# Attention with a two-layer network behind it on one core: first and last pair of a batch in another order, float32 value sums in one batch, other steps for w_out

## The chip, the cores and the metric

The kernel runs on 1 core of one Trainium2 chip. The metric is the device time of one execution in microseconds; the number for a kernel is the median of its runs. The times shown for the kernel before are 1271.4, 1273.9 and 1270.87 us, median 1271.4.

## The reference

Inputs are q, k, v of 8 batches, 12 heads, 448 rows, 64 columns, and the weights w_in (768 x 2048) and w_out (2048 x 768), all float32.

```python
scores = scale * np.matmul(q, k.transpose(0, 1, 3, 2)) - np.log(S)   # scale = 1/sqrt(64)
attn = 1.0 / (1.0 + np.exp(-scores))
x = np.matmul(attn, v).transpose(0, 2, 1, 3).reshape(B * S, H * D)
h = x @ w_in
g = np.where(h > 0.0, h, np.exp(np.minimum(h, 0.0)) - 1.0)
out = g @ w_out
```

So each head's scores go through a sigmoid, not a softmax, the heads' sums stand side by side as 768 columns for each of 3584 tokens, and a layer pair with the ELU function follows.

## The kernel before, in words

**Numbers as pairs of words.** Matrix products run in float16 with two words a number: `split` (L121 on ScalarE, L122 on VectorE) writes hi = float16(scaled source) and lo = float16(scaled source − hi). A product is then the sum of three: hi·hi, lo·hi, hi·lo. The scales are powers of two, found from a maximum: VectorE takes a maximum by row (`absmax`, L125), puts it on a diagonal `dg` (L105), TensorE spreads the diagonal over all partitions by a product with ones (`pb`, L110), and VectorE reduces that (`al`, L112 and on). In `magnitude`, the part up to `dg` is issued at once and the part from `pb` on is returned as `rest`, to be issued later.

**Work of a batch.** A batch is 6 pairs of heads (hp 0 to 5; n = 6 b + hp numbers all pairs) and then the network's first layer. Batches are numbered from 0. For each pair: `load_qk` and `load_v` (DMAs issued by SyncE into `raw` and `rv`), `prepare` (maxima, `dg`), its `second` part (`pb` and the scales `sc`), its `third` part (`transposed`: splits q and k to `nat`, a DMA transpose into `qk`, splits v to `vn`), `scores` of 4 tiles g (L384; tiles 0 to 2 have 128 keys, tile 3 has the last 64), `soften` (sigmoid to `sg`, L395, then for tiles 0 to 2 the two words `at`, L413 on ScalarE and L414 on VectorE), `values` (sum over keys into `pav`, L433 in words, L425 in float32 for the last tile), `finish` (two words of the result into `xh`). Tiles 0 and 1 and tiles 2 and 3 share two PSUM buffers `psc`, so the scores of tile 2 wait until the sigmoid of tile 0 is through, and those of tile 3 for tile 1. Then `hidden`: `rescale`, and `moe1` with 16 tiles f of 18 products (`ph`, L499), the exponential on ScalarE (L511), and the words of g. The change of ScalarE's function table between exponential and sigmoid is an instruction on ScalarE.

**Batch 0 and the weights.** Batch 0 takes its attention in float32 throughout. Its instructions are ordered by a scheduler. Beside it w_in is loaded and turned into words; beside its `moe1` the same goes on for w_out, by `load_w_out`, a generator of 64 steps: for each half i of the columns 16 load steps (DMA of one tile `so` or `wo`, L226; conversion by L138 and L142 on ScalarE, L143 and L157 on VectorE; a product with ones for the tile's maximum, `so`, L150) and 16 split steps (L121 and L122). `W_OUT = 4` steps stand behind each tile f from 2 on and one more behind the last: 57 steps. The other 7 stand in batch 1: three in each of pairs 0 and 1, the rest in pair 2. `step(n)` takes n of them. Tiles that can't be loaded into a part of `wo` that is still free go to three buffers `so` (tag `at`, which later holds the words of the attention).

**Batches 1 to 7** are written out by hand: on TensorE, ScalarE, VectorE and SyncE instructions stand in the order of the program; only GpSimd's are scheduled. TensorE waits in its order, so whatever stands behind a waiting instruction waits too. The second layer of the batch before (`moe2`: tiles `po` of 16 steps, a step is three products of 384 columns, L529) fills the places where the attention would wait: `fill(n)` takes n steps. There are 96 steps in odd batches and 128 in even ones (with the left-over rows of two batches), and each pair's share is what is left, divided by the pairs left. The row of a pair is: scores and soften of tiles 0 and 1, `third` of the next pair, loads of pair n+3, a gap of 5 steps (8 in pair 0), `prepare` of pair n+2, scores and soften of tiles 2 and 3, the rest of the share, `second` of pair n+2, values, finish. In the last pair (hp 5) `hidden` starts ahead of the fill, and 4 steps of the share, the tail, stand behind finish, ahead of `moe1`.

Of the kernel before, what the change touches and what calls it, by code (L numbers as in the profile page):

```python
# [32 lines left out]
def attention_ffn(  # L33
# [25 lines left out]
    SKEW = 2  # L59
    W_IN = [1, 3, 6, 9, 12, 15, 16]  # L60
    W_LOAD = [1, 1]
    W_OUT = 4
    assert 2 * D == P and 2 * R == P and NK == NP

    const = ctx.enter_context(tc.tile_pool(name="const", bufs=1))
# [54 lines left out]
    def split(hi, lo, src, s):  # L120
        nc.scalar.mul(hi, src, s)  # L121
        nc.vector.scalar_tensor_tensor(lo, src, s, hi, op0=ALU.mult, op1=ALU.subtract)  # L122
# [5 lines left out]
    def words(st):  # L128
        w = st.bitcast(U32).rearrange("p a (c t) -> p a c t", t=2)
        return w[:, :, :, 0], w[:, :, :, 1], st  # L130
# [71 lines left out]
    def load_w_out(wo):  # L202


        for i in range(NH):
            whole = [
                wo[:, i, f + SKEW].rearrange("p j c -> p (j c)").bitcast(F32)
                for f in range(NF - SKEW)
            ] + [
                sb.tile([P, HM], F32, tag="o", name=f"to{i}_{f}", bufs=OB) for f in range(SKEW)  # L210
            ]
            sums = ps.tile([P, 512], F32, tag="pm", name=f"so{i}", bufs=3)
            for f in range(NF):

                if i == 0 and f >= 2:
                    st = wo[:, 1, f % 8 * 2 :][:, :2]
                elif i == 1 and f % 2 and f < NF - SP - SKEW:
                    st = wo[:, 1, NF - SP + f // 2 % 2 * 2 :][:, :2]
                else:
                    st = None  # L220
                if st is None:

                    st = sb.tile([P, 1, HM], U64, tag="at", name=f"so{i}_{f}", bufs=AB)
                else:
                    st = st.rearrange("p a j c -> p (a j c)").bitcast(U64).unsqueeze(1)
                nc.sync.dma_start(  # L226
                    st[:, 0], w_out[f * P : (f + 1) * P, i * HM : (i + 1) * HM]
                )
                lo, hi, hl = words(st)
                t = whole[f].unsqueeze(1)  # L230
                magnitudes(t, lo, hi, hl, sums[:, :HM], f == 0, f == NF - 1)
                signed(t, hi)
                yield
            sum_magnitude(wop[:, i : i + 1], sums[:, :HM])
            s = sb.tile([P, 1 + NF], F32, tag="swo", name=f"swo{i}", bufs=2)
            nc.vector.reciprocal(s[:, 0:1], wop[:, i : i + 1])
            nc.vector.tensor_scalar(s[:, 1:], wn, s[:, 0:1], None, op0=ALU.mult)
            for f in range(NF):
                split(wo[:, i, f, 0], wo[:, i, f, 1], whole[f], s[:, 1 + f : 2 + f])
                yield  # L240
# [53 lines left out]
    def prepare(b, hp, raw, rv, xs):  # L294


        u = f"{b}_{hp}"
        n = 1 if b < EXACT else 3
        mx = sb.tile([P, 3], F32, tag="mx", name=f"mx{u}", bufs=2)
        absmax(mx[:, 0:1], rv.rearrange("p t d -> p (t d)"))  # L300
        if n > 1:
            mt = sb.tile([P, 2, NC + 1], F32, tag="mt", name=f"mt{u}", bufs=2)
            absmax(
                mt.rearrange("p i t -> p (i t)")[:, : 2 * NC + 1],
                raw.rearrange("p t h d -> p t (h d)"),
            )
            nc.vector.tensor_reduce(mx[:, 1:3], mt[:, :, :NC], axis=AX.X, op=ALU.max)
            for i, r in enumerate(rows):
                m = mx[r, 1 + i : 2 + i]
                nc.vector.tensor_tensor(m, m, mt[r, 0, NC:], op=ALU.max)  # L310
        pw = sb.tile([P, n], F32, tag="pw", name=f"pw{u}", bufs=2)
        product = magnitude(pw, mx[:, :n], n)

        def scales():
            product()
            sc = sb.tile([P, n + 3], F32, tag="sc", name=f"sc{u}", bufs=3)
            if b >= EXACT:
                nc.vector.reciprocal(sc[:, :n], pw)
                nc.gpsimd.tensor_scalar(sc[:, :n], sc[:, :n], 2.0**TOP, None, op0=ALU.mult)

                for i, r in enumerate(rows):
                    nc.gpsimd.tensor_copy(sc[r, n + 1 : n + 2], sc[r, 1 + i : 2 + i])

                nc.gpsimd.tensor_scalar(  # L324
                    sc[:, n + 2 :], pw[:, 1:2], pw[:, 2:3], 2.0 ** (-2 * TOP) / math.sqrt(D),
                    op0=ALU.mult, op1=ALU.mult,
                )
            value_scale(b, hp, pw[:, 0:1], sc[:, n : n + 1], xs)
            return lambda: transposed(sc)

        def transposed(sc):
            x_scale, s_rest, s_scale = (sc[:, n + i : n + i + 1] for i in range(3))
            if b < EXACT:
                pt = ps.tile([P, 2, 512], F32, tag="psc", name=f"pt{u}", bufs=2)
                pt = pt.rearrange("p a x -> p (a x)")
                for t in range(2 * NC + 1):
                    nc.tensor.transpose(
                        pt[:, t * P : (t + 1) * P], raw[:, t].rearrange("p h d -> p (h d)"), ident
                    )
                qk = early[:, hp % 2]  # L340
                nc.vector.tensor_copy(qk, pt[:, : 2 * S])
                return x_scale, 1 / math.sqrt(D), [qk], ([rv], rv[:, 2 * NC :])
            nat = sb.tile([P, 2, 2 * NC + 1, P], F16, tag="nat", name=f"nat{u}")
            for t, n_t, s in (
                (0, NC, sc[:, 1:2]), (NC, 1, s_rest), (NC + 1, NC, sc[:, 2:3])
            ):
                split(
                    nat[:, 0, t : t + n_t], nat[:, 1, t : t + n_t],
                    raw[:, t : t + n_t].rearrange("p t h d -> p t (h d)"), s,
                )  # L350
            qk = sb.tile([P, 2, 2 * NC + 1, P], F16, tag="qk", name=f"qk{u}", bufs=2)
            nc.sync.dma_start_transpose(
                qk.rearrange("p i t x -> p (i t) x"), nat.rearrange("p i t x -> p (i t x)")
            )
            parts = [qk[:, i].rearrange("p t x -> p (t x)") for i in range(2)]

            vn = sb.tile([P, 2, 2 * NC, D], F16, tag="vn", name=f"vn{u}", bufs=2)
            split(vn[:, 0], vn[:, 1], rv[:, : 2 * NC], sc[:, 0:1])
            vr = sb.tile([P, 2, D], F32, tag="vr", name=f"vr{u}", bufs=2)
            nc.gpsimd.tensor_scalar(  # L360
                vr, rv[:, 2 * NC :], sc[:, 0:1], 2.0**ATOP, op0=ALU.mult, op1=ALU.mult
            )
            return x_scale, s_scale, parts, ([vn[:, 0], vn[:, 1]], vr)

        return scales

    class Pair:
# [23 lines left out]
        def soften(self, g):  # L391
# [6 lines left out]
            if b - 1 in last_exp:  # L398
# [5 lines left out]
                    ),  # L404
                    reason="one change of tables each way for a batch",
                )
            if b < EXACT or g == NC:

                self.sg[g] = [sg]
                return  # L410
# [205 lines left out]
    def w_out_beside(f):  # L616
        nonlocal wo, steps
        if f == 0:
            w_in_ratios()
            wo = sb.tile([P, NH, NF, 2, HM], F16, tag="wo", name="wo")  # L620
            steps = load_w_out(wo)
        if f >= 2:
            step(W_OUT)
        if f == NF - 1:
            step(1)

    def pair_of(n):
        b, hp = pairs[n]
# [56 lines left out]
    with tc.manual_schedule(engines={E.PE, E.Activation, E.DVE, E.SP}):  # L685
        for b in range(EXACT, B):
# [9 lines left out]

            for hp in range(NP):
                n = b * NP + hp
                share = left // (NP - hp)
                tail = 4 if hp == NP - 1 else 0  # L700
                p = pair_of(n)
                for t in range(2):
                    p.scores(t)
                    p.soften(t)
                third()
                if n + 3 < len(pairs):
                    loaded[n + 3] = load_qk(*pairs[n + 3]), load_v(*pairs[n + 3])

                gap = 8 if hp == 0 else 5
                fill(gap)  # L710
                second = prepare_pair(n + 2)
                for t in range(2, NC + 1):
                    p.scores(t)
                    p.soften(t)
                if b == EXACT and hp < NC:

                    step(3 if hp < NC - 1 else NF)
                if hp == NP - 1:
                    h = hidden(b)
                    next(h)  # L720
                fill(share - gap - tail)
                third = second()
                for t in range(NC + 1):
                    p.values(t)
                p.finish()
                fill(tail)
                if b == EXACT and hp == NC - 1:
                    out_scale(*of_moe2, slice(1, NH))
            of_moe2 = next(h)
# [33 lines left out]
```

## Time and profile before

| what | value |
|---|---|
| median of the three runs | 1271.4 us |
| the profiled execution's own time | 1270.86 us |
| its span in the profile | 1269.1 us |
| TensorE busy (instructions) | 1200.2 us (7246) |
| VectorE busy | 823.4 us (1872) |
| ScalarE busy | 671.8 us (1015) |
| GpSimd busy | 84.1 us (319) |
| HBM read, written | 58.20 MB, 11.01 MB |

The span starts with the first instruction in the profile and ends with the last; 1.8 us of the execution's time lie outside it. In the profile PE is TensorE, DVE VectorE, ACT ScalarE, POOL GpSimd and SP SyncE; PEld is TensorE's loading of weights, beside its products. A row of a timeline gives the start, the busy time, the engine, the line of the code, the operation, output and inputs with their partitions and elements, the number of such instructions in a row (x24), and in square brackets the idle time of the engine ahead of them with the instruction that ended it. A row of waits gives the waiting instruction, the one it waited for, the total in us, how many times, and the longest. A row of the windows gives the stretch, its length, busy time and instructions of PE, PEld, DVE, ACT and POOL, the clock that TensorE was granted as a share of full speed, the busy share of the DMA engines and GB/s. SPq rows are DMAs as SyncE issued them; the row of a DMA group ends with the KB of one and the median us from issue to landing.

### The profile page before, as it was taken

Reading aid. Unit: us, or ns where it says so; the run is one execution under the profiler, and the core shown is the slowest. Engines: PE = TensorE matmul, PEld = TensorE weight load, DVE = VectorE, ACT = ScalarE, POOL = GpSimd, SP = SyncE. Lnnn points to the kernel's source line nnn. Section 1 sums busy time; section 2 is a strip of 40 time slices with the busy share of each in tenths; the row PEclk is TensorE's granted clock in tenths of the full one; section 3 lists DMA queues with packets and bytes.
Section 4 is the critical chain, followed back from the end, with each engine's and each line's share of the span. In section 5 each row is a group of like instructions: output and inputs, shape, how many; then the busy total and the mean of one; then the engine's idle time right before and its main releaser. Section 6 shows DMA issues by size and latency. Waiting matters only on the chain.

```text
span 1269.1 us, 19337 instructions
## 1 busy us (share of the span) xinstructions
PE 1200.2 (95%) x7246; PEld 610.5 (48%) x7246; DVE 823.4 (65%) x1872; ACT 671.8 (53%) x1015; POOL 84.1 (7%) x319
## 2 busy tenths in 40 slices
PE   5979868999999999999999999999999999999998
PEld 2324334445555554545455554545455554455565
DVE  5898989765766557775666646885576656765500
ACT  5867777643655337744555436654565435663400
POOL 0011001100000000010000000010000100100000
PEclk9889979999999999999999999999999999999999
DMA  8937423420233103340144201440034401410000
GB/s 229 281 100 222 126 77 80 100 49 1 60 84 89 37 1 83 89 86 1 37 92 92 50 1 43 105 103 7 1 86 92 92 1 22 106 43 7 1 25 26
DMA packets 213407, 89.76 MB, mean 71 GB/s; under 512 B 177472, under 2 KB 209216, under 8 KB 213312
## 3 DMA queue, kind: packets, MB, share of 16 engines
q1 hardware_dynamic: 213312, 88.51, 28.7%
q8 instruction: 57, 0.93, 0.3%
q14 instruction: 38, 0.31, 0.1%
HBM read 58.20 MB, written 11.01 MB: 55 GB/s over the span
## 4 chain that ended last, share of the span: by engine, by line
PE 78%; ACT 8%; DVE 7%; DMA 3%; issue 2%; SPq 2%; DVEq 0%; POOL 0%; ACTq 0%; POOLq 0%
PE ph L499 31%; PE po L529 25%; PE psc L384 7%; PE pav L433 6%; PE po_r L529 5%; PE pav L425 3%; ACT sg L395 2%; DMA stage<-in_moe_w_in_dram 2%; ACT at L413 1%; SPq L262 1%; PE pb L110 1%; ACT L395 1%; ACT e L511 1%; DVE e L514 1%; DMA so<-in_moe_w_out_dram 1%
## 5 line engine op out<-in xcount | busy, mean ns | idle before, releaser
L499 PE MATMUL ph<-xh,wi 128*128 128x448 f16 x2304 | 442.0, 353 | 6.1 <-DVE xh L122 2.4
L529 PE MATMUL po<-wo,g 128*128 128x384 f16 x2304 | 392.9, 328 | 0.0
L529 PEld LDWEIGHTS <-g 128*128 128x128 f16 x2688 | 257.2, 98 | 198.4 <-issue 36.3
L499 PEld LDWEIGHTS <-wi 128*128 128x128 f16 x2304 | 225.3, 98 | 218.4 <-issue 7.6
L511 ACT ACTIVATE e<-ph,msc 128x448 f32<-128x448 f32 x128 | 80.8, 633 | 211.7 <-PE ph L499 211.6
L414 DVE SCALAR_TENSOR_TENSOR at<-sg,at 128x896 f16<-128x896 f32 x126 | 137.2, 1090 | 84.5 <-ACT at L413 84.5
L395 ACT ACTIVATE sg<-psc,bias,sc 128x896 f32<-128x896 f32 (+1 forms) x168 | 166.6, 992 | 1.7
L513 DVE TENSOR_SCALAR e<-e 128x448 f32<-128x448 f32 x128 | 50.3, 394 | 170.8 <-ACT e L511 170.7
L121 ACT ACTIVATE xh<-pav,sc 128x448 f16<-128x448 f32 x48 | 30.3, 632 | 216.7 <-PE pav L425 216.7
L384 PE MATMUL psc<-qk 64*128 64x448 f16 x1008 | 116.6, 355 | 11.4 <-ACT sg L395 11.4
L413 ACT ACTIVATE at<-sg 128x896 f16<-128x896 f32 x126 | 119.8, 951 | 4.1
L121 ACT ACTIVATE g<-e,msc 128x384 f16<-128x384 f32 (+1 forms) x192 | 96.0, 534 | 6.0 <-DVE e L514 4.3
L122 DVE SCALAR_TENSOR_TENSOR g<-e,msc,g 128x384 f16<-128x384 f32 (+1 forms) x192 | 94.6, 521 | 0.6
L514 DVE SCALAR_TENSOR_TENSOR e<-ph,msc,e 128x448 f32<-128x448 f32 x128 | 87.3, 683 | 4.0
L384 PEld LDWEIGHTS <-qk 64*128 64x128 f16 x1008 | 41.7, 97 | 89.7 <-issue 60.2
L433 PE MATMUL pav<-at,vn 128*64 128x448 f16 x756 | 80.2, 357 | 0.0
L324 POOL TENSOR_SCALAR sc<-pw 128x1 f32<-128x1 f32 x42 | 12.4, 295 | 843.5 <-DVE pw L114 790.9
L529 PE MATMUL po_r<-wo,g 128*128 128x384 f16 x384 | 64.7, 326 | 0.0
L122 DVE SCALAR_TENSOR_TENSOR xh<-pav,sc,xh 128x448 f16<-128x448 f32 x48 | 32.7, 680 | 48.7 <-ACT xh L121 48.7
L433 PEld LDWEIGHTS <-vn 128*64 128x64 f16 x756 | 39.4, 110 | 50.0 <-issue 27.8
L122 DVE SCALAR_TENSOR_TENSOR nat<-raw,sc,nat 128x384 f16<-128x384 f32 (+1 forms) x126 | 59.1, 524 | 0.0
L121 ACT ACTIVATE nat<-raw,sc 128x384 f16<-128x384 f32 (+1 forms) x126 | 58.8, 529 | 0.0
(103 smaller groups left out, 852.7 us busy)
## 6 DMA issues: line engine op xcount, KB each, us to landing
stage<-in_moe_w_in_dram SPq DMA_DIRECT2D x16, 768.0 KB, 6.6
raw<-in_q_dram SPq DMA_DIRECT2D x96, 96.0 KB, 3.1
raw<-in_k_dram SPq DMA_DIRECT2D x96, 96.0 KB, 2.6
rv<-in_v_dram SPq DMA_DIRECT2D x48, 192.0 KB, 2.7
out_dram<-o SPq DMA_DIRECT2D x48, 192.0 KB, 2.1
wo<-in_moe_w_out_dram SPq DMA_DIRECT2D x19, 384.0 KB, 4.1
so<-in_moe_w_out_dram SPq DMA_DIRECT2D x13, 384.0 KB, 4.3
raw<-in_q_dram SPq DMA_DIRECT2D x48, 32.0 KB, 2.4
```

The costliest lines, as they stand in the source:

```text
L121: nc.scalar.mul(hi, src, s)
L122: nc.vector.scalar_tensor_tensor(lo, src, s, hi, op0=ALU.mult, op1=ALU.subtract)
L384: nc.tensor.matmul(psc[:, j, :S] if g < NC else psc[rows[j], 0, :S], kk[rows[j], o], qq[rows[j], :S], start=(n == 0), stop=(n == len(parts ...
L395: a = nc.scalar.activation(sg[:, :nb], psc[:, :nb, :S], AF.Sigmoid, bias=bias, scale=self.s_scale)
L413: nc.scalar.mul(hi, sg, 2.0**ATOP)
L414: nc.vector.scalar_tensor_tensor(lo, sg, 2.0**ATOP, hi, op0=ALU.mult, op1=ALU.subtract)
L433: nc.tensor.matmul(pav[rows[j], :S], vv[i][:, j * NC + g], sg[k][:, j], start=(g == 0 and n == 0), stop=False,)
L499: nc.tensor.matmul(ph[:, :S], wi[:, wj, c, f * P : (f + 1) * P], xh[:, c, xj], start=(n == 0), stop=(n == 3 * NK - 1),)
L511: a = nc.scalar.activation(e, ph[:, :S], AF.Exp, scale=inv)
L513: nc.vector.tensor_scalar(e, e, 1.0, -1.0, op0=ALU.min, op1=ALU.add)
L514: nc.vector.scalar_tensor_tensor(e, ph[:, :S], inv, e, op0=ALU.mult, op1=ALU.max)
L529: nc.tensor.matmul(po[:, :HM], lh(gj, f), wo[:, i, f, wj], start=(n == 0), stop=(n == 3 * NF - 1),)
```

## The change

It has four parts, in the diff below without its repeated lines.

- **w_out.** `W_OUT` is 3 and the extra step is gone: 42 steps stand in batch 0 and 22 in batch 1 (four after the gap and four after tiles 2 and 3 in pairs 0 and 1; four and the rest in pair 2). The load of a tile is issued two steps ahead of its conversion.
- **Values of batch 1.** For b = 1 the sigmoid stays float32, v is scaled by ScalarE alone into float32 `vn`, and `values` takes one product a half (6 a pair, recorded as 12) instead of three (18). No `at` is written there.
- **Pair 0 of each batch.** Its share has three steps more and its gap is 11. `prepare` of pair n+2 stands behind scores and soften of tiles 2 and 3, and its `second` (with `pb`) in the next pair, between the scores and the soften of tiles 0 and 1.
- **Last pair.** There is no tail: the whole share stands ahead of `second` and values.

By the share's rule odd batches now take 19, 15, 15, 15, 16, 16 steps and even ones 24, 20, 21, 21, 21, 21.

```diff
-    W_OUT = 4
+    W_OUT = 3
...
+            def load(f):
...
                 nc.sync.dma_start(
                     st[:, 0], w_out[f * P : (f + 1) * P, i * HM : (i + 1) * HM]
                 )
-                lo, hi, hl = words(st)
+                return st
+
+            staged = [load(f) for f in range(2)]
+            for f in range(NF):
+                if f + 2 < NF:
+                    staged.append(load(f + 2))
+                lo, hi, hl = words(staged[f])
...
+            if b == EXACT:
+                s_whole = sb.tile([P, 1], F32, tag="s2", name=f"s2{u}", bufs=2)
+                nc.gpsimd.tensor_scalar(s_whole, sc[:, 0:1], 2.0**ATOP, None, op0=ALU.mult)
+                vn = sb.tile([P, 2 * NC, D], F32, tag="vn", name=f"vn{u}", bufs=2)
+                nc.scalar.mul(vn, rv[:, : 2 * NC], s_whole)
+                return x_scale, s_scale, parts, ([vn], vr)
...
-            if b < EXACT or g == NC:
+            if b <= EXACT or g == NC:
...
-        if f == NF - 1:
-            step(1)
...
-                share = left // (NP - hp)
-                tail = 4 if hp == NP - 1 else 0
+                share = left // (NP - hp) + (3 if hp == 0 else 0)
                 p = pair_of(n)
                 for t in range(2):
                     p.scores(t)
+                if hp == 1:
+                    third = second()
+                for t in range(2):
                     p.soften(t)
                 third()
...
-                gap = 8 if hp == 0 else 5
+                gap = 11 if hp == 0 else 5
                 fill(gap)
-                second = prepare_pair(n + 2)
+                if b == EXACT and hp < NC:
+
+                    step(4)
+
+                if hp:
+                    second = prepare_pair(n + 2)
                 for t in range(2, NC + 1):
                     p.scores(t)
                     p.soften(t)
+                if not hp:
+                    second = prepare_pair(n + 2)
                 if b == EXACT and hp < NC:
-
-                    step(3 if hp < NC - 1 else NF)
+                    step(4 if hp < NC - 1 else NF)
...
-                fill(share - gap - tail)
-                third = second()
+                fill(share - gap)
+                if hp:
+                    third = second()
                 for t in range(NC + 1):
                     p.values(t)
                 p.finish()
-                fill(tail)
```

Two places where this moves instructions. The first is SyncE's row at the start of batch 1; `so` are tiles of w_out, `qk_1` is the transpose for pair 1, `raw_3` and `rv` are q, k and v of pair 3. Before:

```order
L226 DMA so_11_1476<-in_moe_w_out_dram 128x384
L226 DMA so_12_1507<-in_moe_w_out_dram 128x384
L226 DMA so_13_1514<-in_moe_w_out_dram 128x384
L226 DMA so_14_1521<-in_moe_w_out_dram 128x384
L226 DMA so_15_1528<-in_moe_w_out_dram 128x384
L352 DMA_TRANSPOSE qk_1_1648<-nat_1_1641 128x14x128
L262 DMA raw_3_1655<-in_q_dram 128x3x64 x2
L266 DMA raw_3_1655<-in_q_dram 64x2x64
L262 DMA raw_3_1655<-in_k_dram 128x3x64 x2
L266 DMA raw_3_1655<-in_k_dram 64x2x64
L247 DMA rv_85<-in_v_dram 128x2x192
L252 DMA rv_85<-in_v_dram 64x64 x2
```

And now, in the changed kernel:

```order
L227 DMA so_11_1540<-in_moe_w_out_dram 128x384
L359 DMA_TRANSPOSE qk_1_1580<-nat_1_1573 128x14x128
L269 DMA raw_3_1588<-in_q_dram 128x3x64 x2
L273 DMA raw_3_1588<-in_q_dram 64x2x64
L269 DMA raw_3_1588<-in_k_dram 128x3x64 x2
L273 DMA raw_3_1588<-in_k_dram 64x2x64
L254 DMA rv_85<-in_v_dram 128x2x192
L259 DMA rv_85<-in_v_dram 64x64 x2
L227 DMA so_12_1632<-in_moe_w_out_dram 128x384
L227 DMA so_13_1639<-in_moe_w_out_dram 128x384
L227 DMA so_14_1646<-in_moe_w_out_dram 128x384
L227 DMA so_15_1653<-in_moe_w_out_dram 128x384
```

The loads of the tiles 12 to 15 have moved from ahead of the transpose of pair 1 to behind it and behind the loads of pair 3.

The second place is VectorE's row in pair 0 of batch 3; the number behind a name's first underscore is the pair: `mx_2`, `mt_2` and `pw_2` belong to the preparation of pair 2, `at_0` and `xh` to pair 0. Before:

```order
L122 SCALAR_TENSOR_TENSOR vn_1_4696<-rv_85,sc_1_4205,vn_1_4696 128x384
L125 TENSOR_REDUCE mx_2_4736<-rv_83 128x1
L125 TENSOR_REDUCE mt_2_4738<-raw_2_4090 128x7
L307 TENSOR_REDUCE mx_2_4736<-mt_2_4738 128x2
L310 TENSOR_TENSOR mx_2_4736<-mx_2_4736,mt_2_4738 64x1 x2
L105 TENSOR_SCALAR dg<-eye,mx_2_4736 128x128 x3
L414 SCALAR_TENSOR_TENSOR at_0_4757<-sg_0_4755,at_0_4757 128x896
L537 TENSOR_SCALAR o_0_0_4793<-po_0_0_4711,osc_4659 128x384
L112 TENSOR_REDUCE al<-pb 128x3
```

Now:

```order
L122 SCALAR_TENSOR_TENSOR vn_1_4578<-rv_85,sc_1_4101,vn_1_4578 128x384
L427 SCALAR_TENSOR_TENSOR at_0_4634<-sg_0_4632,at_0_4634 128x896
L125 TENSOR_REDUCE mx_2_4646<-rv_83 128x1
L125 TENSOR_REDUCE mt_2_4648<-raw_2_3973 128x7
L314 TENSOR_REDUCE mx_2_4646<-mt_2_4648 128x2
L317 TENSOR_TENSOR mx_2_4646<-mx_2_4646,mt_2_4648 64x1 x2
L105 TENSOR_SCALAR dg<-eye,mx_2_4646 128x128 x3
L550 TENSOR_SCALAR o_0_0_4673<-po_0_0_4591,osc_4539 128x384
L122 SCALAR_TENSOR_TENSOR xh_3810<-pav_0_4686,sc_0_3903,xh_3810 128x448
L125 TENSOR_REDUCE xs_3811<-xh_3810 128x1
L112 TENSOR_REDUCE al<-pb 128x3
```

The words of the third tile (`at_0`) have moved ahead of the maxima and `dg`, and the reduction of `pb` behind the end of the pair (`xh`).

More of the change, by code (lines that the diff above doesn't have):

```diff
@@ L212, in load_w_out @@
             sums = ps.tile([P, 512], F32, tag="pm", name=f"so{i}", bufs=3)
-            for f in range(NF):
+            def load(f):
                 if i == 0 and f >= 2:
@@ L355, in transposed @@
             parts = [qk[:, i].rearrange("p t x -> p (t x)") for i in range(2)]
-            vn = sb.tile([P, 2, 2 * NC, D], F16, tag="vn", name=f"vn{u}", bufs=2)
-            split(vn[:, 0], vn[:, 1], rv[:, : 2 * NC], sc[:, 0:1])
             vr = sb.tile([P, 2, D], F32, tag="vr", name=f"vr{u}", bufs=2)
@@ L362, in transposed @@
             )
+            if b == EXACT:
[4 more added lines that the diff above has]
+                return x_scale, s_scale, parts, ([vn], vr)
+            vn = sb.tile([P, 2, 2 * NC, D], F16, tag="vn", name=f"vn{u}", bufs=2)
+            split(vn[:, 0], vn[:, 1], rv[:, : 2 * NC], sc[:, 0:1])
             return x_scale, s_scale, parts, ([vn[:, 0], vn[:, 1]], vr)
```

## The prediction

> **What bounds the kernel now.** I read the page first: the busy times and the shares of the chain that ended last.
>
> ```profile
> PE 1200.2 (95%) x7246; PEld 610.5 (48%) x7246; DVE 823.4 (65%) x1872; ACT 671.8 (53%) x1015; POOL 84.1 (7%) x319
> ...
> PE 78%; ACT 8%; DVE 7%; DMA 3%; issue 2%; SPq 2%; DVEq 0%; POOL 0%; ACTq 0%; POOLq 0%
> ```
>
> PE is busy for 1200.2 us of the 1269.1 us span, so about 69 us of it are idle, and 78% of the chain is PE's own work. The change removes no PE work in the steady part; it can only remove PE waits, and it may add some. So the next view is PE's waits in the window 268 to 1148 us (the stages of batches 2 to 7; batches are numbered from 0, pairs of a batch too):
>
> ```profile
> PE pb L110 <- DVE dg L105: 9.7, 5, 2.0
> PE psc L384 <- ACT sg L395: 6.7, 6, 1.2
> ```
>
> That is 16.4 us in eleven waits. PE's timeline shows where they stand:
>
> ```profile
> 260.77 0.32 PE L110 MATMUL pb<-dg,ones 128*128 128x384 bf16 x1 [1.90 <-DVE dg L105]
> ...
> 474.24 4.07 PE L529 MATMUL po<-wo,g 128*128 128x384 f16 x24
> ...
> 480.01 0.76 PE L384 MATMUL psc<-qk 64*64 64x448 f16 x6 [1.03 <-ACT sg L395]
> ...
> 486.75 0.32 PE L110 MATMUL pb<-dg,ones 128*128 128x384 bf16 x1 [1.97 <-DVE dg L105]
> ...
> 494.92 5.54 PE L529 MATMUL po<-wo,g 128*128 128x384 f16 x33
> 500.40 0.32 PE L110 MATMUL pb<-dg,ones 128*128 128x384 bf16 x1
> ```
>
> The psc wait (480.01) stands once in each of the six batches, in its first pair: the eight gap steps (24 po matmuls) don't last until the sigmoid of the second tile is through. The pb wait stands in the first pair of batches 3, 5, 7 (486.75) and in the last pair of odd batches (260.77 is batch 1's, ahead of the window). A step is three po matmuls; the 33 that start at 494.92 fill the time up to 500.40, so one step is 5.48/11 = 0.50 us.
>
> **The change part by part.**
>
> *Waits that go.* In the first pair the gap grows from 8 to 11 steps: 1.5 us more cover, over waits of 1.2 at most. The row max and dg now stand behind the second half of the sigmoids on DVE, and pb moves into the next pair, behind its first scores, several us after dg. The first pair also takes three steps more, so values find their operands. In the last pair the four tail steps move ahead of pb: 4 x 0.50 = 2.0 us of cover over waits of 1.90. All three kinds go: 6.7 + 9.7 + 1.9 = −18.3 us.
>
> *What is late next.* Three steps more in the first pair, and four that no longer trail the last one, leave less for the others: by the share rule the odd batches' pairs take 19, 15, 15, 15, 16, 16 steps where all took 16; even batches 24, 20, 21 and on. Pair 1 of batch 3, whose second fill is the 33 po at 494.92, has 16 steps, and there DVE's row reads:
>
> ```profile
> 499.77 0.58 DVE L105 TENSOR_SCALAR dg<-eye,mx 128x128 bf16<-128x128 bf16 x3
> ```
>
> dg ends at 500.35 and pb starts at 500.40: no slack, with DVE the later one. One step less and PE arrives 0.50 early and waits it out: three pairs (1 to 3) in each of batches 3, 5, 7: 9 x 0.50 = +4.5. With 20 or 21 steps an even batch has 2 us in hand. In the last pair the tail also covered the end of the stage:
>
> ```profile
> 265.11 0.67 DVE L122 SCALAR_TENSOR_TENSOR xh<-pav,sc,xh 128x448 f16<-128x448 f32 x1
> ```
>
> ```profile
> 265.65 3.57 PE L499 MATMUL ph<-xh,wi 128*128 128x448 f16 x18
> ```
>
> The last operand of the next matmuls, xh, was ready (265.78) about when ph started. Without the tail ph starts as soon as values end, and xh of the last pair is read only by the last 3 of 18 matmuls, 15 x 3.57/18 = 3.0 us in. xh follows the end of values by some 1.4 to 3 us in these rows, so the end is covered within a few tenths. I put +1.0 on these edges over all batches. Together +5.5 us; bounds 0 (DVE work pulled ahead by the same amount) and +9.
>
> *float32 values in batch 1.* The saved low word's split and the two forms of the values' sum:
>
> ```profile
> L414 DVE SCALAR_TENSOR_TENSOR at<-sg,at 128x896 f16<-128x896 f32 x126 | 137.2, 1090 | 84.5 <-ACT at L413 84.5
> ```
>
> ```profile
> 45.09 2.48 PE L433 MATMUL pav<-sg,rv 128*64 128x448 f32 x12
> ...
> 206.38 1.89 PE L433 MATMUL pav<-at,vn 128*64 128x448 f16 x18
> ```
>
> A pair drops three L414, 3 x 1.09 = 3.3 us of DVE, and their three first words on ACT, which once w_out is done nothing on PE waits for. PE pays 2.48 − 1.89 = 0.59 a pair, x6 = +3.5 us. The first row is batch 0's form at full clock, which batch 1 will issue. At half clock a group would cost up to twice as much, bound +10. The Trainium skill, page "FP8 and Floating Point Precision", section TensorE Precision Notes, says that true FP32 takes 4 passes through the array; 24 passes against 18 would be an estimate of 1.89 x 24/18 = 2.52, in this kernel +3.8, which speaks against this part of the change by 0.3 us more. The row decides.
>
> *Pair 1 of batch 1.* Before, twelve splits of w_out stood ahead of its sigmoids on ACT:
>
> ```profile
> 196.46 0.74 PE L384 MATMUL psc<-qk 64*128 64x448 f16 x6 [2.51 <-ACT sg L395]
> 198.43 1.17 PE L384 MATMUL psc<-qk 64*64 64x448 f16 x6 [1.23 <-ACT sg L395]
> 199.53 6.75 PE L529 MATMUL po<-wo,g 128*128 128x384 f16 x33
> ```
>
> Now the first steps there follow scores and sigmoids. The waits of 2.51 and 1.23 go, and with them the slow spell that makes 33 po take 6.75 instead of 5.54: −2.5 − 1.2 − 1.2 = −4.9. If the splits only move to pair 2 some of it returns: bounds −4.9 and 0.
>
> *Pair 0 of batch 1.* This is the disputed place. Before:
>
> ```profile
> 168.69 0.80 PE L150 MATMUL so<-wo,ones 128*128 128x384 bf16 x2 [1.42 <-DVE wo L143]
> 170.15 0.33 PE L150 MATMUL so<-wo,ones 128*128 128x384 bf16 x1 [0.67 <-DVE wo L143]
> 175.79 0.48 PE L150 MATMUL so<-wo,ones 128*128 128x384 bf16 x1 [5.30 <-DVE wo L143]
> 177.67 0.48 PE L150 MATMUL so<-to,ones 128*128 128x384 bf16 x1 [1.41 <-DVE to L143]
> 178.73 0.48 PE L150 MATMUL so<-to,ones 128*128 128x384 bf16 x1 [0.58 <-DVE to L143]
> 180.17 1.33 PE L384 MATMUL psc<-qk 64*64 64x448 f16 x6 [0.96 <-ACT sg L395]
> 181.43 5.80 PE L529 MATMUL po<-wo,g 128*128 128x384 f16 x24
> ```
>
> Idle: 1.42 + 0.67 + 5.30 + 1.41 + 0.58 + 0.96 = 10.3 us, on the loads of so_12 and later. In the order of instructions these loads stood on SP ahead of the transpose of pair 1; now so_12 to so_15 stand behind it and behind the loads of pair 3:
>
> ```profile
> 183.70 1.56 SPq L352 DMA_TRANSPOSE qk<-nat  x1
> ...
> 190.48 1.14 SPq L252 DMA_DIRECT2D rv<-in_v_dram  x2
> ```
>
> ```profile
> so<-in_moe_w_out_dram SPq DMA_DIRECT2D x10, 384.0 KB, 3.8
> ```
>
> From the transpose's start to the end of the last rv issue SP takes 191.62 − 183.70 = 7.9 us. Call T0 the end of batch 0's last ph. The transpose needs nat, whose splits follow two sigmoids on ACT; without the w_out work between them I put nat at T0 + 6, so so_12 is issued at T0 + 14 and lands at T0 + 18. PE has 11 steps (5.5 us) until its four so matmuls, then waits in order: some 13 us, 1.1 for the next tile's conversion (178.73 − 177.67) and 3.0 for so_15, whose buffer is so_12's and whose load goes out only then. That is 17.2, +6.9 against before; the half clock that follows such a gap is there before too (24 po in 5.80). Bounds: 0 and +11.
>
> *End of batch 0.* Two conversions fewer stand among its last tiles, and one wait of PE with the half clock behind it can go:
>
> ```profile
> 152.93 0.50 PE L150 MATMUL so<-wo,ones 128*128 128x384 bf16 x2 [2.07 <-DVE wo L143]
> ```
>
> I take −2, bounds −4 and 0.
>
> **Sum:** −18.3 + 5.5 + 3.5 − 4.9 + 6.9 − 2.0 = −9.3. The profiled execution took 1270.86 us (span 1269.1); the median of the three runs is 0.5 higher, 1271.4. So 1271.4 − 9.3 = 1262.1, predicted as 1262.
>
> **The rivals.**
>
> *The loads ahead work* (chance 0.08). If so_12 to so_14 are issued early enough that they are there when their step comes, pair 0 waits no longer than before: the term +6.9 becomes about 0, 1255. For it: the change does load two tiles ahead. Against: on SP these loads stand behind the transpose whichever tile they belong to. The Trainium skill, page "Trainium Kernel Development and Optimization", section Best Practices, advises to double-buffer so that DMA overlaps with compute; by it this would be the case, and no run here shows it for these loads.
>
> *Half clock through two pairs* (slower, 0.06). After the long gap in pair 0 the granted clock stays at half. Before:
>
> ```profile
> 181.00:185.00 4.00, 4.00 (x16) 1.72 (x13) 4.00 (x10) 3.97 (x8) 1.76 (x5) 0.50 0.03 7
> 185.00:188.00 3.00, 3.00 (x23) 1.68 (x23) 2.94 (x11) 1.62 (x3) 0.47 (x2) 1.00 0.93 182
> ```
>
> It came back 3.6 us after PE set off at 181.43. If instead float32 sums and small waits kept it at half over both pairs, about 25 us of PE work would take up to 23 more: 1278 to 1285. It decides from some 15 us of work at half clock (1262 + 15 = 1277). Against it is the quick return in these two rows. The Trainium skill, page "TensorE: Matmul & The Clock Gate", section What's actually happening, has the clock return after about 3.4 us of sustained work; the rows agree.
>
> *The gains are eaten in batch 1 and by the shares* (same, 0.13). Pair 0 at +11, shares at +9, values at half clock in part (+6): −18.3 + 9 + 6 − 4.9 + 11 − 2 = +0.8, some 1272; with two of the three, 1266 to 1270.
>
> *A part doesn't do what it says* (0.03, also same): the pb wait comes back in the next pair, because dg still isn't there; then 9.7 of the gain stays out and 1271 results. Against: scores and a whole block of values lie between.
>
> **How the numbers follow.** The forecast, 1258 to 1267, has 0.70. 0.3% of 1271.4 is 3.8 us, about what a measurement of this kernel can tell from no change: faster means below 1267.6. Faster: 0.70 + 0.08 and a little of the eaten case, 0.80; same 0.14; slower 0.06. The range takes in the loads that work and most of the eaten case: 1254 to 1270.
>
> **What would show it.** Right: in the profile after, no psc or pb wait in first and last pairs from batch 2 on; pb waits of some 0.5 in pairs 1 to 3 of batches 3, 5, 7; values of batch 1 at 2.5 a group; one PE gap of over 10 us in front of so in batch 1's pair 0, with SP's loads of so behind the transpose. Wrong: no such gap (then faster); no pb waits in the short pairs; half clock in batch 1 far past the gap.

## The result and the profile after

The changed kernel takes 1263.67 us in the median of 4 runs (1262.40 to 1265.79), the kernel before 1272.62 us (4 runs): ratio 0.9932, 95% interval 0.9910 to 0.9954. That is 8.95 us less, against 9.3 forecast. Run once more later, beside other kernels, it gave 0.9922 (0.9907 to 0.9938). One execution of a kernel below, the one with float32 values alone, took 3143.12 us and is left out of that kernel's ratio.

The page of the profile after (1264.65 us, span 1262.8), the rows that answer to those shown of before:

```profile
PE 1200.0 (95%) x7210; PEld 606.9 (48%) x7210; DVE 804.7 (64%) x1848; ACT 654.8 (52%) x997; POOL 94.5 (7%) x325
...
PE 72%; DVE 10%; ACT 7%; DMA 4%; issue 3%; SPq 2%; POOL 1%; DVEq 0%; ACTq 0%; POOLq 0%
```

PE's busy time has not moved (1200.2 to 1200.0). What the change gave is less waiting, and VectorE now carries 10% of the chain instead of 7%. PE's waits over batches 2 to 7 (window 271 to 1145 us):

```profile
PE pb L110 <- DVE dg L105: 5.2, 9, 1.1
PE psc L397 <- DMA qk<-nat: 1.0, 1, 1.0
```

All eleven waits of before (16.4 us) are gone; ten others of 6.2 us in all stand in their place. The nine pb waits are those of pairs 1 to 3 in batches 3, 5 and 7; the psc wait stands in pair 1 of batch 7. PE's timeline of batch 3, pairs 1 to 5:

```profile
503.64 0.32 PE L110 MATMUL pb<-dg,ones 128*128 128x384 bf16 x1 [1.12 <-DVE dg L105]
517.29 0.32 PE L110 MATMUL pb<-dg,ones 128*128 128x384 bf16 x1 [0.44 <-DVE dg L105]
530.94 0.32 PE L110 MATMUL pb<-dg,ones 128*128 128x384 bf16 x1 [0.43 <-DVE dg L105]
544.59 0.32 PE L110 MATMUL pb<-dg,ones 128*128 128x384 bf16 x1
558.25 0.32 PE L110 MATMUL pb<-dg,ones 128*128 128x384 bf16 x1
```

The last of these is the last pair, without a wait where the one of 1.9 was. Batch 1 is the other side of the account. PE's timeline of its pair 0 and of the end of pair 1 (a `so` row is the product with ones for the maximum of a tile of w_out):

```profile
163.24 5.05 PE L542 MATMUL po<-wo,g 128*128 128x384 f16 x30 [1.47 <-DVE e L527]
...
173.83 0.48 PE L150 MATMUL so<-wo,ones 128*128 128x384 bf16 x1 [4.88 <-DVE wo L143]
175.42 0.48 PE L150 MATMUL so<-wo,ones 128*128 128x384 bf16 x1 [1.12 <-DVE wo L143]
182.72 0.48 PE L150 MATMUL so<-wo,ones 128*128 128x384 bf16 x1 [6.82 <-DVE wo L143]
184.32 0.48 PE L150 MATMUL so<-wo,ones 128*128 128x384 bf16 x1 [1.12 <-DVE wo L143]
184.72 2.56 PE L397 MATMUL psc<-qk 64*128 64x448 f16 x12
189.56 0.33 PE L150 MATMUL so<-to,ones 128*128 128x384 bf16 x1 [2.27 <-DVE to L143]
191.00 0.48 PE L150 MATMUL so<-to,ones 128*128 128x384 bf16 x1 [1.12 <-DVE to L143]
191.28 5.43 PE L542 MATMUL po<-wo,g 128*128 128x384 f16 x24
196.63 2.48 PE L446 MATMUL pav<-sg,vn 128*64 128x448 f32 x12
...
211.75 0.32 PE L110 MATMUL pb<-dg,ones 128*128 128x384 bf16 x1 [1.40 <-DVE dg L105]
```

Pair 0 waits 1.47 + 4.88 + 1.12 + 6.82 + 1.12 + 2.27 + 1.12 = 18.8 us, before 10.3. The 6.82 are a wait for a load, that of tile 12: ScalarE, which converts the tiles, stands idle for it just as long.

```profile
181.11 0.54 ACT L138 ACTIVATE wo<-so 128x384 f32<-128x384 f32 x1 [6.79 <-DMA so<-in_moe_w_out_dram]
```

The value sums take 2.48, as forecast. Pair 1 has lost its two sigmoid waits and has a new pb wait of 1.40.

From the first and last ph of each batch in PE's timelines, the length of each attention stage in us (from the last ph of one batch to the first of the next):

| batch | before | after | new order alone | last of the experiments |
|---|---|---|---|---|
| 1 | 103.47 | 109.83 | 101.45 | 100.52 |
| 2, 4, 6 | 98.0 | 96.73 | 96.73 | 96.73 |
| 3 | 86.87 | 83.79 | 83.83 | 83.45 |
| 5 | 88.46 | 83.79 | 83.83 | 83.80 |
| 7 | 84.37 | 83.61 | 83.27 | 83.26 |

The last two columns are kernels of the next section. So batch 1 lost 6.4 us and batches 2 to 7 gained 12.4. Batch 5 gained 1.6 more than batch 3 with the same work: the profile of before has a spell of half clock there, right behind the pb wait of 1.97 us in pair 0. The windows of before show it in the second row (PEclk is the number ahead of the last two):

```profile
778.00:782.00 4.00, 2.03 (x16) 0.99 (x16) 3.87 (x11) 1.59 (x3) 0.00 (x0) 1.00 0.70 138
782.30:785.70 3.40, 3.40 (x14) 1.02 (x12) 1.38 (x7) 0.00 (x0) 1.12 (x5) 0.50 0.57 127
786.00:790.00 4.00, 4.00 (x33) 1.88 (x27) 2.30 (x3) 3.85 (x5) 0.15 (x1) 1.00 0.18 58
```

The two profiled executions differ by 6.2 us and the medians by 8.95: that of before lies 1.8 below its median and that of after 1.0 above. Sums made from the traces below answer to the 6.2.

### The profile page after: what moved, and what is told of

It reads as the page before. It is cut to its first block, busy times and chain, and to the rows that moved or that the text cites. A ratio compares the mean times of both kernels' runs of the same rounds, so it can differ in the third digit from the quotient of the medians.

```text
span 1262.8 us, 19227 instructions
## 1 busy us (share of the span) xinstructions
PE 1200.0 (95%) x7210; PEld 606.9 (48%) x7210; DVE 804.7 (64%) x1848; ACT 654.8 (52%) x997; POOL 94.5 (7%) x325
## 4 chain that ended last, share of the span: by engine, by line
PE 72%; DVE 10%; ACT 7%; DMA 4%; issue 3%; SPq 2%; POOL 1%; DVEq 0%; ACTq 0%; POOLq 0%
PE ph L512 30%; PE po L542 20%; PE psc L397 6%; PE pav L446 6%; PE po_r L542 5%; PE pav L438 3%; ACT sg L408 3%; DMA stage<-in_moe_w_in_dram 2%; DVE mt L125 1%; DMA wo<-in_moe_w_out_dram 1%; ACT at L426 1%; SPq L269 1%; DVE nat L122 1%; DVE mx L125 1%; DVE dg L105 1%
## 5 line engine op out<-in xcount | busy, mean ns | idle before, releaser
L427 DVE SCALAR_TENSOR_TENSOR at<-sg,at 128x896 f16<-128x896 f32 x108 | 117.6, 1089 | 74.3 <-ACT at L426 74.0
L426 ACT ACTIVATE at<-sg 128x896 f16<-128x896 f32 x108 | 102.6, 950 | 3.4
L446 PE MATMUL pav<-at,vn 128*64 128x448 f16 x648 | 68.2, 355 | 0.0
L550 DVE TENSOR_SCALAR o<-po,osc 128x384 f32<-128x384 f32 x48 | 29.4, 612 | 48.3 <-PE po L542 43.5
```

What stands on the lines that cost most here:

```text
L426: nc.scalar.mul(hi, sg, 2.0**ATOP)
L427: nc.vector.scalar_tensor_tensor(lo, sg, 2.0**ATOP, hi, op0=ALU.mult, op1=ALU.subtract)
L446: nc.tensor.matmul(pav[rows[j], :S], vv[i][:, j * NC + g], sg[k][:, j], start=(g == 0 and n == 0), stop=False,)
```

## The experiments

Theory A: the gain is the waits that the new order removes, and what the other two parts lose in batch 1 is TensorE standing, in its order, at products of w_out tiles that aren't ready. The rivals are named in the expectations. Every kernel was timed against the kernel before on the same chip; the medians of before were 1272.1, 1273.5 and 1272.4 us in the three sets, so ratios are compared.

### The new order alone

`load_w_out`, its steps and the values as before; the rest as in the change.

```diff
-    W_OUT = 3
+    W_OUT = 4
...
-            if b <= EXACT or g == NC:
+            if b < EXACT or g == NC:
```

> The kernel before with only the new order of pair 0 and the last pair (gap 11, three steps more, maxima behind tiles 2 and 3, pb in the next pair, no tail). Theory A (the gain is the waits that this order removes): 10.8 us over batches 2 to 7 and about 1.5 in batch 1, so some 12 us faster than before, 1260 to 1261, faster than the whole change. Theory B (the gain comes from w_out's steps and the float32 values, the order only exchanges one pb wait for three short ones): within 3 us of before.

1257.75 us, ratio 0.9880 (0.9865 to 0.9895): faster than the whole change. The gain on before, 14.3 us, is some 2 us more than theory A's figure; the half clock of batch 5 (1.6 us) is gone here too. Theory B falls. Which step of the order removes which wait was not tried one by one, apart from the shares below. The even batches gain the same as in the change, and batch 1 gains 2.0 where the change loses 6.4. PE's waits in batch 1 (window 160 to 272 us):

```profile
PE so L150 <- DVE wo L143: 6.7, 2, 6.0
PE psc L394 <- ACT sg L405: 5.2, 3, 3.0
PE pb L110 <- DVE dg L105: 1.4, 3, 0.5
PE so L150 <- DVE to L143: 1.1, 2, 0.6
```

They come to 14.4 us; in the change the same window has 13.9 + 3.4 at so, 1.7 at pb and 1.5 at po, 20.5 in all, and the float32 sums on top.

### The float32 values alone

```diff
-            if b < EXACT or g == NC:
+            if b <= EXACT or g == NC:
...
+                vn = sb.tile([P, 2 * NC, D], F32, tag="vn", name=f"vn{u}", bufs=2)
+                nc.scalar.mul(vn, rv[:, : 2 * NC], s_whole)
```

> The kernel before with only the float32 values of batch 1. The values cost 6 x 0.59 = 3.5 us. Without words of the attention in the shared buffers, three loads of w_out stand behind the transpose and the loads of pair 3 on SP. Theory A: the wait in pair 0 of batch 1 grows from 10.3 to some 15 us, 7 to 9 us slower than before. Theory B: ScalarE and VectorE are relieved of 36 splits in batch 1, which shortens the waits in pairs 0 and 1 by 4 us or more: no slower than before.

1272.22 us, ratio 0.9995 (0.9985 to 1.0006): no change that can be measured. Theory A falls here. The time is theory B's, but not by its account: pair 0 waits 3.6 us instead of 10.3, pair 1 waits 9.0 instead of 3.7, and the last pair's 1.9 is gone. In pairs 0 and 1 that is 1.5 us less where theory B had 4 or more; with the last pair it is 3.4, about what the float32 sums cost, and the stage takes 103.45 us against 103.47. One group of sums fell into half clock (4.17 instead of 2.48). PE's timeline of pairs 0 and 1:

```profile
176.52 4.17 PE L443 MATMUL pav<-sg,vn 128*64 128x448 f32 x12
...
195.24 2.56 PE L394 MATMUL psc<-qk 64*128 64x448 f16 x12 [7.44 <-ACT sg L405]
```

Three loads of w_out stand behind the transpose here too, but their products stand behind pair 0's value sums (from 182.81 us on), so pair 0 does not wait for them. The w_out work had moved on and held the sigmoids of the next pair instead, in ScalarE's order behind twelve splits.

### The change without its new order

```diff
-                share = left // (NP - hp) + (3 if hp == 0 else 0)
+                share = left // (NP - hp)
+                tail = 4 if hp == NP - 1 else 0
...
-                gap = 11 if hp == 0 else 5
+                gap = 8 if hp == 0 else 5
```

(`prepare_pair`, `second` and `fill(tail)` stand where they stood before, too.)

> The change without its new order: w_out's steps, loads two ahead and float32 values of batch 1 on the old order of pairs. Theory A: +8.5 in pair 0 of batch 1, +3.5 for the values, -3.7 in pair 1, -0.8 in batch 0: 6 to 8 us slower than before, about 1280. Theory B: 6 to 9 us faster than before.

1274.31 us, ratio 1.0017 (1.0007 to 1.0026): slower by 2, less than theory A said, and far from theory B. Batch 1's stage takes 109.31 us, 5.8 more than before, where theory A's terms come to 8.3; 1.9 of the difference is the last pair's pb wait, which is gone. Batch 0's first layer took 69.7 us in this profile against 73.04, which gives 3.4 back.

The two halves don't add: −14.3 for the order and +2.2 for the rest would be −12.1, the change has −9.0. The order's 2.0 us in batch 1 are missing in the change. There the last pair's pb wait of 1.9 is gone without the new order (no pb wait stands in batch 1 of this kernel, nor of the one with float32 values alone), so the order finds nothing to remove, and its short pairs cost 1.7 (1.40 + 0.29). In the profiles batch 0 adds to it: it ends 4.05 us earlier than before in this kernel, 0.75 in the change; why is open (last section).

### w_out's loads ahead of the transpose

In pair 0 of batch 1 the four conversion steps, and with them the loads, are issued ahead of `third`.

```diff
+                early_steps = b == EXACT and hp == 0
+                if early_steps:
+                    fill(gap)
+                    step(4)
                 third()
```

> The change with the four conversion steps of batch 1's pair 0 (and with them the loads of tiles 12 to 15) ahead of the transpose of pair 1 and of the loads of pair 3. Theory A (the place of these loads on SP makes the wait of 18.8 us in that pair): the wait falls to about 8 us, 9 to 11 us faster than the change, about 1254. Theory C (the three shared buffers make it: a load can only go out when a tile is converted): the wait stays above 15 us and the time within 4 us of the change.

1258.35 us, ratio 0.9888 (0.9875 to 0.9902). Both expectations missed: 5 us less than the change, where A said 9 to 11 and C under 4. In the change SyncE issued the loads of so_12 and on behind the others; its rows there:

```profile
169.61 1.55 SPq L359 DMA_TRANSPOSE qk<-nat  x1
...
176.38 1.13 SPq L259 DMA_DIRECT2D rv<-in_v_dram  x2
177.56 6.63 SPq L227 DMA_DIRECT2D so<-in_moe_w_out_dram  x4
```

And PE's timeline with the loads ahead of the transpose:

```profile
160.88 5.05 PE L542 MATMUL po<-wo,g 128*128 128x384 f16 x30 [1.53 <-DVE e L527]
...
170.94 0.48 PE L150 MATMUL so<-wo,ones 128*128 128x384 bf16 x1 [4.35 <-DVE wo L143]
172.53 0.48 PE L150 MATMUL so<-wo,ones 128*128 128x384 bf16 x1 [1.12 <-DVE wo L143]
174.13 0.48 PE L150 MATMUL so<-wo,ones 128*128 128x384 bf16 x1 [1.12 <-DVE wo L143]
176.84 0.48 PE L150 MATMUL so<-wo,ones 128*128 128x384 bf16 x1 [2.23 <-DVE wo L143]
...
182.53 0.48 PE L150 MATMUL so<-to,ones 128*128 128x384 bf16 x1 [2.71 <-DVE to L143]
184.12 0.48 PE L150 MATMUL so<-to,ones 128*128 128x384 bf16 x1 [1.12 <-DVE to L143]
```

The wait of 6.82 for so_12's load has become 1.12, so the load's place on SP made that wait; other waits grew by 1.1, and pair 0 has 4.6 us less in all, the stage 4.1 (105.76 against 109.83). But 14.2 us of 18.8 are still waited: the first product waits 4.35 for a tile that had long been loaded, since on ScalarE its conversion (at 169.32 us) stands behind the change of the function table (162.00), two sigmoids and what is left of batch 0. And each tile takes 1.60 us (172.53 to 174.13), since VectorE's sign step waits for the product and the next tile's conversion stands behind it.

### The steps later

The change, with two conversions at the end of pair 0, two in pair 1 ahead of the transpose, two at its end, and the sixteen splits in pair 2.

```diff
+                ahead = b == EXACT and hp == 1
+                if ahead:
+                    fill(gap)
+                    step(2)
                 third()
...
-                if b == EXACT and hp < NC:
-                    step(4)
+                if b == EXACT and hp == 2:
+                    step(8)
...
-                if b == EXACT and hp < NC:
-                    step(4 if hp < NC - 1 else NF)
+                if b == EXACT and hp == 2:
+                    step(NF)
...
                 fill(share - gap)
+                if b == EXACT and hp < 2:
+                    step(2)
```

> The change with batch 1's w_out steps later: two conversions at the end of pair 0, two in pair 1 ahead of the transpose, two at its end, all sixteen splits in pair 2. Theory A (what is lost in pair 0 is TensorE held, in its order, at products whose tile is not yet loaded and converted): the wait of 18.8 us falls to 2 to 4, a few us come back in pairs 2 and 3 behind the splits, 1250 to 1253. Theory E (the conversions cost their time wherever they stand, since ScalarE or VectorE bound batch 1): the waits move to pairs 1 to 3 and the time is within 3 us of the change.

1256.84 us, ratio 0.9860 (0.9846 to 0.9875), 4 us above theory A's range and 7 below the change; theory E falls for the conversions. The splits moved with them, so the gain is that of both moves. PE's timeline:

```profile
162.43 5.05 PE L542 MATMUL po<-wo,g 128*128 128x384 f16 x30 [0.29 <-DVE e L527]
...
171.06 0.65 PE L542 MATMUL po<-wo,g 128*128 128x384 f16 x3 [0.81 <-DVE wo L122]
172.66 0.65 PE L542 MATMUL po<-wo,g 128*128 128x384 f16 x3 [0.94 <-DVE wo L122]
173.85 3.94 PE L542 MATMUL po<-wo,g 128*128 128x384 f16 x14 [0.54 <-DVE mx L317]
177.62 0.33 PE L150 MATMUL so<-wo,ones 128*128 128x384 bf16 x1
179.07 0.33 PE L150 MATMUL so<-wo,ones 128*128 128x384 bf16 x1 [1.11 <-DVE wo L143]
...
215.41 0.48 PE L110 MATMUL pb<-dg,ones 128*128 128x384 bf16 x1 [4.50 <-DVE dg L105]
215.82 4.75 PE L446 MATMUL pav<-sg,vn 128*64 128x448 f32 x12
```

Pair 0 waits 0.29 + 0.81 + 0.94 + 0.54 + 1.11 = 3.7 us instead of 18.8, as theory A said, and the stage falls from 109.83 to 101.78. What came back is 2.9 at the `so` products of pair 1, and in pair 2 a wait of 4.50 behind the splits with sums at half clock, 4.75 instead of 2.48.

### Even shares

Pair 0's three extra steps are taken out; the first on the change, the second on the new order alone, the third on the later steps.

```diff
-                share = left // (NP - hp) + (3 if hp == 0 else 0)
+                share = left // (NP - hp)
```

> The change with pair 0's three extra steps taken out of its share: odd batches take 16 steps in each pair, even ones 21 or 22. Theory A (the short pairs of 15 steps wait for dg because VectorE is the later one by just one step): the pb waits of 5.2 us in batches 3, 5, 7 go, and the time falls by some 5 us against the change, to 1258 or 1259. Theory D (pair 0 needs its 19 steps, since its values come after the third tile's words): as much wait comes back in pair 0 and the time stays at 1263.

1263.02 us, ratio 0.9914 (0.9901 to 0.9927); the change had 0.9932 and 0.9922, and the intervals overlap: theory D's time. PE's waits in batches 2 to 7 (window 275 to 1150 us):

```profile
PE pb L110 <- DVE dg L105: 2.1, 3, 0.7
PE pav L446 <- DVE at L427: 1.7, 3, 0.6
PE psc L397 <- DMA qk<-nat: 1.0, 3, 0.3
```

The pb waits fall from 5.2 to 2.1: those of pairs 2 and 3 go, as theory A has it, and pair 1 still waits 0.7. The values of pair 0 now wait for VectorE's words (three times 0.6), and the scores of pair 1 for the transpose. In all 4.8 us against 6.2, so theory D's "as much" is more than came back there; batch 1's stage took 0.8 more (110.62).

> The new order alone, w_out's steps and values as before, with 16 steps in each pair of an odd batch. Theory A: the pb waits of the short pairs, 6.0 us in batches 3, 5, 7 and 1.4 in batch 1, go: 1251 to 1252. Theory D: as much comes back in pair 0: 1257 to 1258.

1257.28 us, ratio 0.9870 (0.9852 to 0.9888) against 0.9880: the same, theory D's time again.

> Both: w_out's steps of batch 1 later and even shares. Theory A: 1245 to 1248. Theories D and E: 1258 to 1264.

1259.30 us, ratio 0.9881 (0.9865 to 0.9898): no gain on the later steps' 0.9860 either, and within the range of theories D and E. In the profile the shares cost here: batch 1's stage takes 106.46 us instead of 101.78. With three steps fewer in pair 0 the `so` products there wait 1.24 and 1.12, and the value sums of pairs 0 to 2 take 4.75, 4.17 and 4.06 instead of 2.48, 2.48 and 4.75. This suggests that the later steps' gain rests in part on pair 0's extra steps; one profile doesn't show it.

### The change again, and the splits spread

> The changed kernel once more, beside the next two: 8 to 9 us faster than before, as measured.

1262.38 us, ratio 0.9922 (0.9907 to 0.9938).

The later steps with the splits over pairs 2 and 3:

```diff
-                if b == EXACT and hp == 2:
-                    step(8)
+                if b == EXACT and hp in (2, 3):
+                    step(4)
...
-                if b == EXACT and hp == 2:
-                    step(NF)
+                if b == EXACT and hp in (2, 3):
+                    step(4 if hp == 2 else NF)
```

> As the kernel with the later w_out steps, but its sixteen splits spread over pairs 2 and 3. Theory A: the pb wait of 4.5 us in pair 2, and the half clock that makes its value sums 4.75 instead of 2.48, go: 5 to 7 us less than with all splits in pair 2, about 1251. Theory E (VectorE bounds batch 1 as a whole): the wait comes back in pair 3 or 4, 1256 to 1257.

1253.77 us, ratio 0.9851 (0.9835 to 0.9867), against 0.9860 with all in pair 2: not told apart. The pb wait fell from 4.50 to 1.88, and new ones came at po in pair 3; PE's timeline there:

```profile
213.18 0.32 PE L110 MATMUL pb<-dg,ones 128*128 128x384 bf16 x1 [1.88 <-DVE dg L105]
213.43 3.75 PE L446 MATMUL pav<-sg,vn 128*64 128x448 f32 x12
...
227.60 0.32 PE L542 MATMUL po<-wo,g 128*128 128x384 f16 x1 [0.92 <-ACT wo L121]
229.44 2.32 PE L542 MATMUL po<-wo,g 128*128 128x384 f16 x11 [1.52 <-DVE wo L122]
```

The stage takes 101.47 instead of 101.78. The time lies between the two expectations (1251; 1256 to 1257): the wait comes back in pair 3, as theory E says of the splits, but that VectorE bounds batch 1 as a whole is not shown.

And the same with words again for the values of pairs 4 and 5:

```diff
-            if b <= EXACT or g == NC:
+            if b < EXACT or (b == EXACT and self.hp < 4) or g == NC:
```

> As that, with the values of batch 1's last two pairs in words again (18 float16 products instead of 6 float32 ones). The float32 form costs 0.59 us a pair on TensorE and nothing else hangs on it there: 1 us less than with float32 in all six. If the words' splits on VectorE bind in those pairs: no less, or 1 us more.

1253.31 us, ratio 0.9848 (0.9831 to 0.9866); the stage takes 100.52, 0.95 less than with float32 throughout (1 us was expected, 2 x 0.59). The whole time can't tell a microsecond; the stage shows it. This version beats both kernels: 19.05 us below before, and below the change by intervals that don't touch.

## Why the prediction was right, step by step

**Waits that go: right.** All of −18.3 went, though the 1.9 of batch 1 would have gone without the new order. The even batches show it bare: 98.0 to 96.73, 1.3 us for a wait of 1.22.

**What is late next: right in place, in size partly by luck.** +5.5 was forecast; 6.2 stand there in batches 2 to 7. Pairs 2 and 3 wait 0.44 and 0.43, the 0.5 of the working; pair 1 waits 1.12, as `second` of pair 0 now stands in it, which the working left out. The even shares bear both out: with the step back, pairs 2 and 3 wait no longer and pair 1 still 0.7, but then pair 0 waits for its words. The +1.0 for the edges was another thing than the 1.0 in front of psc, which the profile of the change run again doesn't have: of the edges the first layers of batches 3 and 5 show 0.25 each.

**float32 values: right.** 2.48 a pair, the row of batch 0. The estimate from the 4 passes that the Trainium skill, page "FP8 and Floating Point Precision", section TensorE Precision Notes, states for float32 was 2.52; the trace has 2.48.

**Pair 1 of batch 1: waits right, one overlooked.** 2.51 and 1.23 and the slow spell are gone (30 po in 5.05, full rate). A pb wait of 1.40 came, which the sum hadn't.

**Pair 0 of batch 1: direction right, size 1.6 too small, its cause half right.** 17.2 forecast, 18.8 measured: 17.3 at the `so` products and 1.47 ahead of them, for an `e` of batch 0's last tiles. The "some 13 us" up to so_12 came as 4.88 + 1.12 + 6.82 = 12.8, in two gaps instead of the one of over 10 us that was to show it, since the products of two tiles loaded earlier stand in between. That the size fits is in part luck, as two misses of 2 us cancel: with T0 = 161.43 the transpose went out at 169.61, T0 + 8.2 instead of + 6, and so_12's load at 177.56, T0 + 16.1 instead of + 14; and PE was through its 11 steps at T0 + 7.5 instead of + 5.5. What the working left out stands next in line: issuing the loads ahead of the transpose took only 4.1 to 4.6 us off. The larger part is that TensorE takes its products in order and four of them stood where their tiles could not yet be converted, loaded or not; moving the steps shows it (3.7 left in pair 0, 2.9 in pair 1).

**End of batch 0: too large in this profile.** −2 forecast, −0.75 in the profile (the last ph ends at 161.43 instead of 162.18). The wait of 2.07 went, but one of 2.38 for an `e` came (ph at 154.12). The same code varies by 2.8 us there from profile to profile (last section), so one profile can't tell the term.

**The sum.** In the traces: −0.75 in batch 0, +6.4 in batch 1, −12.4 after it, +0.5 in the first layers of batches 3 and 5: −6.2, as the profiled executions differ. Of batch 1's terms +3.6 was forecast (3.5 − 4.9 + 6.9 − 1.9), 6.4 measured; the rest is +1.6 in pair 0 and +1.7 of pb waits, less 0.5. Batches 2 to 7 were forecast at −16.4 + 5.5 = −10.9, and 1.6 of half clock that no row had priced came on top. The medians' −8.95 is nearer to −9.3 than these terms are: that the number fits so well is in part luck, since batch 0 and batch 1 came out 1.3 and 2.8 us worse than forecast and batches 2 to 7 1.5 better, and the medians lie 2.7 further apart than the two profiled executions.

**The rivals.** The loads two tiles ahead didn't work as such: they stood behind the transpose. The gains were eaten only in part, 6.4 us in batch 1, and in the changed kernel the moved pb stands without a wait in the next pair. Half clock did not last. The windows of the changed kernel, by stretch:

```profile
168.00:184.00 16.00, 2.37 (x9) 0.76 (x8) 8.65 (x17) 8.27 (x18) 0.00 (x0) 0.67 0.56 145
184.00:191.00 7.00, 3.30 (x14) 0.84 (x14) 5.03 (x13) 3.56 (x6) 0.00 (x0) 0.74 0.19 56
191.00:194.00 3.00, 3.00 (x10) 1.42 (x10) 1.74 (x6) 0.57 (x2) 0.98 (x5) 0.50 0.02 5
194.00:197.00 3.00, 3.00 (x19) 1.56 (x18) 1.77 (x3) 0.55 (x2) 1.20 (x2) 0.99 0.05 17
```

The full clock was back 3 us after PE worked without a gap (from 191.28 us on), ahead of the float32 sums.

## What to carry to other kernels

A wait removed is worth its own length only if the engine that was waited for has slack elsewhere in the stage: ask where its next deadline lies, and price that. An instruction that is cheap on the engine that bounds the kernel (here a product of 0.3 us) still holds everything behind it until its operand is there, so put it where the operand is certain, and put the preparing work that nobody yet needs into the stages with slack. Measure the parts of a change apart: here one part gave 14 us and the others took 5 of them back.

## What the hardware showed unexpectedly

A pb wait of 1.97 us cost more than itself. In each of the three profiled kernels with the old order, in one of the three batches 3, 5 and 7, a spell of half clock follows that wait directly and makes the stage 1.6 us longer (88.46 against 86.87 before; 88.49 with float32 values alone; 85.95 against 84.37 in batch 7 of the change without its order). In the ten profiles with the new order, which have no wait of that length there, no stage of batches 2 to 7 has it. That the wait makes the spell is argued from this, not tried. The Trainium skill, page "TensorE: Matmul & The Clock Gate", section What's actually happening, describes a window of about 3.4 us that runs freely; the spell of 3.40 us and its coming in one batch of three agree with it. By the same page of the Trainium skill half clock comes after an idle window of that length; here the waits ahead of these spells were of 1.97 us, and the measurement decides.

Batch 0's first layer, the same code in nine of the profiles (the change twice and seven other kernels), took 71.3 to 72.5 us in six of them and 69.7 to 70.0 in three. What decides that is open.
